# Where the memory values' tail products stand, and when a tile's mean and deviation are taken: a two-part reordering in a layer-interleaved recurrent-memory transformer kernel

## The chip, the cores and the metric

The kernel runs on one core of one Trainium2 chip. The metric is the device time of one execution in microseconds (us). One core has five engines: TensorE (PE, with its weight loads shown separately as PEld), VectorE (DVE), ScalarE (ACT), GpSimd (POOL) and SyncE (SP, which only issues DMAs here). The engines run on their own and meet at semaphores. Each engine takes its instructions in order. TensorE writes its products into PSUM, a memory that this kernel uses as eight banks; ScalarE and VectorE copy them out, and in this program a bank takes new products only when its last reader is done.

## The reference, cut to what matters

Two attention layers with a recurrent memory and two gated MLP layers are stacked, and the weights are shared:

```python
x = x + A(layernorm(x)); x = x + B(layernorm(x))
x = x + A(layernorm(x)); x = x + B(layernorm(x))

# A: 64 segments of 32 rows; each sees 8 memory rows that the segment before it has made
h = concat([mem, xs]); q, k, v = h @ Wq, h @ Wk, h @ Wv        # 16 heads of 256
o = softmax(mask(q k^T * scale)) v @ Wo
mem = o[:8]; outs.append(o[8:])
# B: (relu(x @ W_gate) * (x @ W_up)) @ W_down, 448 -> 1792 -> 448
```

x is 2048 x 448 in bf16. The memory makes A sequential in the segments.

## The kernel before

It works in 70 steps, one segment per step. Chain C1 is the first A layer and C2 the second, six segments behind. In steps 6 to 63 both chains run together, in one set of products ("two-chain steps", 58 of them). B's work for a finished tile of 128 rows is cut into pieces (`fill`) that are dealt out into holes of TensorE. A tile is four segments, so the steps repeat in fours; I call them step 0, 1, 2 and 3 by their number modulo four. C1 ends a tile in step 3, C2 in step 1.

The order within a two-chain step: `G = M h` in bank pairs (TensorE into PSUM, copied out by ScalarE and VectorE); scores `S = G h`; softmax on VectorE and ScalarE; values `vps = B h`; products with the weights (`AT_ps`); memory rows back into `hTr` (`mps`).

Width 448 is 3 x 128 + 64. The last 64 rows are the "tails": a tail product uses only 64 rows of the array, and two of them, from the lower and the upper half, can run at once (eight value tails of 448 columns take 0.20 us below, while fourteen full products of 448 columns take 2.82 us, 0.20 us each). Two tails from different halves must not write one PSUM bank together, so the score tails go in two turns with a fence in between: GpSimd waits for the last score tail of the first turn and writes a token, and TensorE waits for the token.

```python
def pass_on():
    op = nc.gpsimd.memset(token[:], 0.0)
    sync(op, last_of[nc.tensor.engine])      # waits for TensorE's last matmul
    return op.ins.name
...
def dual(g, chains, inG, mid, ...):
    gp.run(inG); G = gp.G
    matmul(SX[:, 0:N], selq[LO], maskb[LO], start=True, ...)    # the mask product
    mid()                                    # one or two relu pieces of B
    ...
    vm.part(0, True)                         # 8 value tails, banks 0 and 1
    for e in range(2):
        for k in range(4):
            x_tails(k, e)                    # score tails: bank SX, half e
            m_tails(k, 1 - e)                # bank SM, the other half
        if not e:
            passed = pass_on()
            vm.part(1, True)                 # 8 value tails, banks 2 and 3
            fence.append(passed)             # the next matmul waits for the token
    ... full score products, softmax, values ...
    end()                                    # a relu piece ("first product" below)
    ... mps, copies into hTr ...
    for c in ends:                           # a tile ends: add its rows into x
        nc.vector.tensor_tensor(x3[:, cc], ps[...], x3[:, cc], op=ALU.add)
    last()                                   # a relu piece ("second product")

# after the step, for a chain whose tile ended
f = FFN(c, t); f.norm()
```

In B:

```python
def norm(self):                              # bn_stats + bn_aggr on VectorE, rstd on GpSimd
    self.stats = ln_stats(self.t, recent.get("hh"))    # behind the last relu product
def rows(self, after):
    self.xn = ln_rows(self.stats, True, after)         # (x - mean) * rstd, twice
    nc.sync.dma_start_transpose(self.xnT[:], ...)      # transposed by DMA
def turn(self):                              # the first piece of B
    if self.xn is None:
        self.rows(recent["G1"])              # behind the first VectorE copy of G
def gate_up(self, f):                        # a relu piece: 28 matmuls
    ...
    recent["ut"] = nc.scalar.copy(ut[:], gu[1][:])
    recent["hh"] = nc.vector.scalar_tensor_tensor(out=self.hh[...], in0=gu[0][:], scalar=0.0,
                                                  in1=ut[:], op0=ALU.max, op1=ALU.mult)   # the "relu product"; it reads the bank of gate
```

`behind(a, b)` only fixes the order of two instructions on one engine. What is not fixed so is ordered by a scheduler when the program is built, and the scheduler also hands out the eight PSUM banks.

## Time and profile before

| | before |
|---|---|
| time, median of the first 3 runs | 1531.71 us (1528.56 to 1534.23) |
| profiled span | 1529.0 us |
| TensorE busy / weight loads busy | 98% / 75% |
| length of steps 0, 1, 2, 3 (mask product to mask product) | 21.92, 24.52, 21.14, 19.47 us |

The page of the kernel before begins with the span and the engines' busy time:

```profile
span 1529.0 us, 88780 instructions
PE 1492.6 (98%) x41744; PEld 1139.1 (75%) x41744; DVE 951.1 (62%) x2202; ACT 603.8 (39%) x1410; POOL 150.1 (10%) x523
```

TensorE is the engine to relieve, but its 98% hides small holes, because the ends of matmuls are modelled. The Trainium skill (Perfetto Trace Analysis, "Identifying the Most-Contended Engine") also says that matmul busy time is not a good measure of how close a kernel is to its limit, and names weight-load busy time as one of two better ones; here weight loads stand at 75%. The waits view shows who waited for whom: total us, times, longest us. Two of its lines belong to this change:

```profile
PEld L138 <- POOL token L145: 22.9, 58, 0.4
PEld L138 <- DMA xnT_1183<-xd_94: 4.0, 5, 1.1
```

The first is the fence, once in each two-chain step. The second are relu pieces that found the transposed rows of a C1 tile not yet landed.

The timeline of the fence in a step 0 whose mask product stands at 724.86 (columns: start, duration, engine, line, operation, out<-in, shapes, count, idle time before and what ended it):

```profile
724.95 1.05 DVE L501 CAST G<-gps 128x480 bf16<-128x480 f32 x2 [1.84 <-PE gps L138]
...
726.96 0.38 PE L138 MATMUL vps<-BT_sb,memTp_81 64*32 64x448 bf16 x8
727.16 0.20 PE L138 MATMUL S_ps<-G,hTr 64*32 64x80 bf16 x1
...
727.20 0.22 PE L138 MATMUL S_ps<-G,hTr 64*32 64x80 bf16 x4
727.23 0.37 PE L138 MATMUL vps<-BT_sb,memTp_81 64*32 64x448 bf16 x8
...
727.54 0.10 POOL L145 MEMSET token<- 128x1 f32 x1 [7.20 <-PE S_ps L138]
727.69 0.21 PE L138 MATMUL S_ps<-G,hTr 64*32 64x80 bf16 x1
```

Eight value tails occupy the array for 0.20 us (726.96 to 727.16). From the first score tail to the release are 0.53 us (727.16 to 727.69), and in this hole stand only eight value tails. G is complete long before, at 726.00.

The timeline of the end of a step 3, in which C1 finishes a tile (put together from the views of the single engines):

```profile
803.81 0.68 DVE L953 TENSOR_TENSOR x_ring<-AT_ps,x_ring 32x256 bf16<-32x256 f32 x2
...
804.94 0.42 DVE L352 SCALAR_TENSOR_TENSOR hh<-gate,ut 128x256 bf16<-128x256 f32 x1 [0.44 <-ACT ut L351]
804.95 0.84 PE L138 MATMUL gps<-hTr,MT_sb 64*128 64x80 bf16 x36
...
805.56 0.42 DVE L352 SCALAR_TENSOR_TENSOR hh<-gate,ut 128x256 bf16<-128x256 f32 x1 [0.19 <-ACT ut L351]
...
805.90 0.62 DVE L264 BATCH_NORM_STATS2 stats<-x_ring 128x6 f32<-128x448 bf16 x1
806.55 0.18 DVE L266 BATCH_NORM_AGGREGATE mv<-stats 128x2 f32<-128x6 f32 x1
...
807.80 0.50 DVE L282 TENSOR_SCALAR xd_94<-x_ring,mv,rstd 128x448 bf16<-128x448 bf16 x1
...
808.68 1.26 SPq L330 DMA_TRANSPOSE xnT_1183<-xd_94  x1
```

The rows are added by 804.49; then VectorE idles 0.44 us until ScalarE delivers `ut`; then come the two relu products, and the statistics only behind both. The DMA leaves 4.87 us after the add began. The 36 G tails of the next step run without a visible wait at 804.95, three bank pairs of twelve. The third pair reuses the bank that the first relu product reads: its second product starts 0.05 us after that relu product ends.

### The profile page before, as it was taken

To read this page: it belongs to the slowest core of one execution; us is meant where nothing else is said; L and a number is where in the kernel's file an instruction comes from. 1 tells how busy PE (TensorE), PEld (TensorE's weight loads), DVE (VectorE), ACT (ScalarE), POOL (GpSimd) and SP (SyncE) were. 2 spreads that over 40 slices of the span, in tenths; PEclk is the share of its full clock that TensorE was granted. 3 is DMA by queue.
4 is the path that set the end of the run, shared out by engine and by line. 5 is a ranking of instruction groups with operands and counts; after the bars stand their busy time and mean duration, and the time that the engine had idled before them with its cause. 6 is when DMAs were issued, how large, how long until landed. Compare 5 with 4: busy or idle time off the path is not lost. (4 is left out here: it accounts for less than half of the span.)

```text
span 1529.0 us, 88780 instructions
## 1 busy us (share of the span) xinstructions
PE 1492.6 (98%) x41744; PEld 1139.1 (75%) x41744; DVE 951.1 (62%) x2202; ACT 603.8 (39%) x1410; POOL 150.1 (10%) x523
## 2 busy tenths in 40 slices
PE   7999999999999999999999999999999999999998
PEld 4577777778777787778778777877778777777775
DVE  6645566666666666666666666666666665666444
ACT  5644333434343343434344343434334343433443
POOL 2001001010100011010100101010001100001000
PEclk9999999999999999999999999999999999999999
DMA  9731001010000100010000100000000000000000
GB/s 237 168 99 35 5 14 14 12 20 13 20 7 15 18 12 21 12 21 13 9 18 15 19 12 20 12 22 6 15 18 12 18 11 15 12 6 14 5 7 9
DMA packets 82798, 39.35 MB, mean 26 GB/s; under 512 B 65176, under 2 KB 81536, under 8 KB 82432
## 3 DMA queue, kind: packets, MB, share of 16 engines
q1 hardware_dynamic: 82400, 33.68, 10.3%
q8 instruction: 326, 5.34, 1.5%
q14 instruction: 40, 0.33, 0.1%
q10 hardware_dynamic: 32, 0.01, 0.0%
HBM read 14.00 MB, written 1.84 MB: 10 GB/s over the span
## 5 line engine op out<-in xcount | busy, mean ns | idle before, releaser
L138 PE MATMUL gps<-hTr,M_sb 128*128 128x80 bf16 (+1 forms) x11760 | 415.3, 198 | 2.1 <-issue 1.9
L138 PEld LDWEIGHTS <-M_sb 128*128 128x128 bf16 x11760 | 405.1, 99 | 7.2 <-issue 2.7
L501 DVE CAST G<-gps 128x480 bf16<-128x480 f32 (+4 forms) x327 | 194.4, 611 | 223.9 <-PE gps L138 223.7
L501 ACT CAST G<-gps 128x480 bf16<-128x480 f32 (+4 forms) x327 | 165.6, 525 | 344.9 <-PE gps L138 344.9
L138 PEld LDWEIGHTS <-hTr 128*32 128x32 bf16 (+2 forms) x8464 | 178.0, 94 | 164.5 <-issue 47.5
L138 PE MATMUL vps<-B_sb,hTr 128*32 128x448 bf16 x4464 | 235.6, 353 | 0.0
L138 PEld LDWEIGHTS <-Wgu 64*128 64x128 bf16 x6272 | 184.1, 94 | 24.4 <-issue 19.3
L425 ACT CAST vox<-vps 128x448 bf16<-128x448 f32 x186 | 96.1, 533 | 181.1 <-PE vps L138 181.1
L352 DVE SCALAR_TENSOR_TENSOR hh<-gate,ut 128x256 bf16<-128x256 f32 x224 | 94.1, 420 | 69.2 <-ACT ut L351 69.2
L425 ACT CAST VOm<-vps 128x448 bf16<-128x448 f32 x251 | 120.5, 526 | 14.8 <-PE vps L138 14.7
L351 ACT CAST ut<-up 128x256 bf16<-128x256 f32 x224 | 83.8, 374 | 70.3 <-PE up L138 70.3
L425 DVE CAST vox<-vps 128x448 bf16<-128x448 f32 x186 | 104.9, 600 | 9.0 <-PE vps L138 9.0
L853 ACT ACTIVATE se<-se 128x320 f32<-128x320 f32 x116 | 54.5, 470 | 129.4 <-DVE se L852 129.4
L138 PE MATMUL gate<-xnT_1182,Wgu 64*128 64x128 bf16 x1568 | 103.5, 216 | 0.9 <-DMA xnT_1182<-xd_93 0.6
L138 PE MATMUL up<-xnT_1182,Wgu 64*128 64x128 bf16 x1568 | 103.6, 216 | 0.0
L138 PE MATMUL gate<-xnT_1183,Wgu 64*128 64x128 bf16 x1568 | 99.1, 216 | 3.8 <-DMA xnT_1183<-xd_94 2.7
L138 PE MATMUL up<-xnT_1183,Wgu 64*128 64x128 bf16 x1568 | 99.2, 216 | 0.0
L138 PEld LDWEIGHTS <-TW 128*32 128x32 bf16 x3712 | 90.7, 97 | 11.1 <-DVE TW L883 0.7
L138 PE MATMUL gps<-hTr,MT_sb 64*128 64x80 bf16 (+1 forms) x3920 | 92.1, 196 | 3.0 <-ACT hTr L946 0.7
L138 PEld LDWEIGHTS <-memTp_81 128*32 128x32 bf16 (+1 forms) x2820 | 67.0, 95 | 36.3 <-issue 1.7
L138 PEld LDWEIGHTS <-memTp_83 128*32 128x32 bf16 (+1 forms) x2820 | 67.2, 95 | 35.1 <-issue 0.6
L138 PE MATMUL dps<-Wd,hh 128*128 128x448 bf16 x448 | 92.7, 354 | 0.0
(194 smaller groups left out, 1730.8 us busy)
## 6 DMA issues: line engine op xcount, KB each, us to landing
wo<-in_A_Wo_dram SPq DMA_DIRECT2D x8, 448.0 KB, 5.1
out_dram<-x_ring SPq DMA_DIRECT2D x16, 112.0 KB, 1.7
Wgu<-in_B_W_gate_dram SPq DMA_DIRECT2D x7, 224.0 KB, 3.3
Wgu<-in_B_W_up_dram SPq DMA_DIRECT2D x7, 224.0 KB, 3.5
Wd<-in_B_W_down_dram SPq DMA_DIRECT2D x7, 224.0 KB, 3.1
wvn_124<-in_A_Wv_dram SPq DMA_DIRECT2D x4, 384.0 KB, 3.5
wvn_125<-in_A_Wv_dram SPq DMA_DIRECT2D x4, 384.0 KB, 5.9
x_ring<-in_A_x_dram SPq DMA_DIRECT2D x10, 112.0 KB, 3.0
```

Source lines behind the costliest of these rows:

```text
L138: op = nc.tensor.matmul(*a, **k)
L351: recent["ut"] = nc.scalar.copy(ut[:], gu[1][:])
L352: recent["hh"] = nc.vector.scalar_tensor_tensor(out=self.hh[:, f:f + 2, :], in0=gu[0][:], scalar=0.0, in1=ut[:], op0=ALU.max, op1=ALU.mult)
L425: op = self.evac[2 * x + e](self.dst[:, 2 * e + x, :], self.ps[x][e][:, 0:DM])
L501: op = (cp_a, cp_v)[self.side](gp.G[:, self.side, self.t0:self.t0 + self.n, gp.c0:gp.c1, :], self.ps[:, 0:self.n * gp.NP].rearrange("p (m ...
L853: vm.after = nc.scalar.activation(se[:, q], se[:, q], AF.Exp, scale=SCALE)
```

## The change

The intent: (A) put both value-tail passes into the hole of the fence. (B) Take the C1 tile's statistics right after the rows are added, make its normalized rows ahead of the next step's first G copy, and so send the transposing DMA earlier.

```diff
 # ln_rows
-            nc.vector.tensor_copy(xd[:, :, 1], xd[:, :, 0])
+            recent["rows"] = nc.vector.tensor_copy(xd[:, :, 1], xd[:, :, 0])
 # FFN.norm
-            self.stats = ln_stats(self.t, recent.get("hh"))
+            self.stats = recent.pop("stats", None) or ln_stats(self.t, recent.get("hh"))
 # Bank.out, first VectorE copy of G
                 if not self.t0:
                     recent["G1"] = op
+                    if ahead_of_G:
+                        behind(op, ahead_of_G.pop())
+    ahead_of_G = []
 # dual
-        vm.part(0, True)
         for e in range(2):
             for k in range(4):
                 x_tails(k, e)
                 m_tails(k, 1 - e)
             if not e:
                 passed = pass_on()
-                vm.part(1, True)
+                vm.both(True)
                 fence.append(passed)
 # dual, behind the add of an ended tile's rows
+            if c is C1:
+                recent["stats"] = ln_stats((g - c.lag) // 4)
 # after the step
                 if c is C2 and recent["two"] and g + 1 < nseg and t:
                     f.rows(recent["sum"])
+                elif c is C1 and recent["two"] and g + 1 < nseg:
+                    f.rows(recent["hh"])
+                    ahead_of_G.append(recent["rows"])
```

## The prediction

> **What bounds it now.** The page: TensorE 98% busy of a 1529.0 us span, weight loads 75%, VectorE 62%, granted clock 0.999. The Trainium skill (Perfetto Trace Analysis, "Identifying the Most-Contended Engine") judges TensorE by weight loads, not matmuls; either way only gaps of its in-order stream can be saved. The waits view gives the two that this change touches: weight loads behind the token, 22.9 us in 58 waits; behind the DMA into xnT_1183, 4.0 us in 5.
>
> **Step A, both tail passes between the turns.** 58 two-chain steps have the fence. The skill (TensorEngine Tiling, "Gotcha 1: PSUM Pressure") says row tiles must not write one bank together: hence the fence; no run here tests it. In the timeline of a step with two relu pieces ahead: value tails start 1.79 us after the mask matmul, first score tails 1.99, second value tails 2.06, token 2.37, release 2.53. The release follows the first score tail by 0.54 us whatever fills it; eight value tails fill only 0.2. Moving the other eight into the hole starts score tails 0.20 earlier. Nothing is removed or added.
> - Steps 0 and 1 of each four (28): G is ready at 1.15, long before. Saved 28 x 0.20 = 5.6 us.
> - Steps 2 and 3 (30): one relu piece. Tails start 1.01, VectorE's last G cast ends 1.15, score tails start 1.21: the eight tails were hiding that cast. The k=3 score tails will now wait for it; saved about 30 x 0.04 = 1.2 us.
> A: -6.8 us, all on TensorE's stream.
>
> **Step B, statistics and rows of a C1 tile earlier.** VectorE work is unchanged: 0.62 + 0.18 us statistics, 0.50 + 0.29 rows. Now the transposing DMA is issued about 3.2 us after the relu product and lands 2.9 to 4.6 us later; where it is late, the relu matmuls wait: five tiles, 3.7 us together beyond the usual. Issued 1.0 to 1.5 us earlier, those waits go: -3.7 us.
> Cost: VectorE is idle only 0.44 us before the first relu product, so the statistics push it 0.15 to 0.37 us. In the timeline the third bank pair's tails of the next step start 0.04 us after this product ends, at its release: no slack. 15 tile ends x 0.15 to 0.37 = 2 to 5.5 us, unless banks are handed out differently; I take +3.5 us. The rows ahead of the first G cast delay it at most 0.3 us; no bank is short there.
> B: about 0.
>
> **Sum.** -6.8 - 3.7 + 3.5 = -7.0 us: 1531.7 to 1525 us, range 1519 to 1530. Faster by over 2%: 1%; within 2%: 98%; slower: 1%.
>
> **What would show it.**
> - A: 16 value tails in one group behind the score tails; mask-to-release 2.53 to 2.33 in steps 0 and 1, 1.74/1.80 to about 1.70/1.76 in steps 2 and 3; wait for the token from 0.39 each to 0.2 and 0.1. Score tails waiting for G's cast in steps 2 and 3 only.
> - B: C1's transposing DMA issued 1.0 to 1.5 us earlier; waits on xnT_1183 from 4.0 to under 0.5 us; the relu product at C1 ends later by 0.15 to 0.37 us, and a TensorE wait of that size before the third pair's tails.
>
> **What would make it wrong.** Token latency depending on the queue ahead (A smaller); PSUM banks handed out in another order, so the product no longer gates tails (B better) or gates earlier ones (B worse); the DMA landing late for another reason; the scheduler placing the statistics after the first product.

## The result

| | before | changed |
|---|---|---|
| time, median of 4 runs | 1531.8 us | 1526.31 us (1525.36 to 1527.48) |
| ratio (95% interval) | | 0.9966 (0.9945 to 0.9986) |
| profiled span | 1529.0 us | 1523.6 us |
| length of steps 0, 1, 2, 3, usual | 21.92, 24.52, 21.14, 19.47 us | 21.73, 24.33, 21.06, 19.73 us |

A ratio is the mean time of one kernel's fast runs over that of the other's in the same rounds, so it isn't quite the ratio of the medians quoted.

Steps 0, 1 and 2 became shorter, step 3 became longer by 0.26 us. Two-chain steps together are 6.8 us shorter (here and below: the 56 from step 6 to step 61, mask product to mask product). The page and the waits of the changed kernel (the second line from the view of TensorE alone):

```profile
span 1523.6 us, 88780 instructions
PE 1494.2 (98%) x41744; PEld 1143.1 (75%) x41744; DVE 952.3 (63%) x2202; ACT 603.8 (40%) x1410; POOL 149.4 (10%) x523
```

```profile
PEld L138 <- POOL token L145: 15.2, 58, 0.3
PE gps L138 <- DVE hh L352: 2.3, 13, 0.2
```

Busy times tell nothing: TensorE is even 1.6 us busier and its weight loads are 4.0 us busier, in a shorter span. The waits tell it. The token costs 15.2 us instead of 22.9. The line for the DMA into xnT_1183 is gone. A new line stands there: G products waiting for a relu product, in 13 steps. The view counts only 0.2 us for each, since earlier matmuls were still modelled as running.

The fence in the same step 0, whose mask product now stands at 723.24:

```profile
723.33 1.06 DVE L501 CAST G<-gps 128x480 bf16<-128x480 f32 x2 [1.84 <-PE gps L138]
...
725.03 0.21 PE L138 MATMUL S_ps<-G,hTr 64*32 64x80 bf16 x1
...
725.07 0.23 PE L138 MATMUL S_ps<-G,hTr 64*32 64x80 bf16 x4
725.11 0.58 PE L138 MATMUL vps<-BT_sb,memTp_81 64*32 64x448 bf16 x16
...
725.42 0.10 POOL L145 MEMSET token<- 128x1 f32 x1 [8.21 <-PE S_ps L138]
...
725.57 0.21 PE L138 MATMUL S_ps<-G,hTr 64*32 64x80 bf16 x1
```

The score tails lead, 16 value tails stand in one group behind them, and first score tail to release is 0.54 us again (725.03 to 725.57). From the mask product to the release it is 2.33 us; in a step 0 without a late DMA it was 2.53.

The end of a step 3 in the changed kernel:

```profile
801.35 0.68 DVE L955 TENSOR_TENSOR x_ring<-AT_ps,x_ring 32x256 bf16<-32x256 f32 x2
...
802.06 0.63 DVE L264 BATCH_NORM_STATS2 stats<-x_ring 128x6 f32<-128x448 bf16 x1
802.48 0.63 PE L138 MATMUL gps<-hTr,MT_sb 64*128 64x80 bf16 x25
...
802.73 0.18 DVE L266 BATCH_NORM_AGGREGATE mv<-stats 128x2 f32<-128x6 f32 x1
802.83 0.74 DVE L352 SCALAR_TENSOR_TENSOR hh<-gate,ut 128x256 bf16<-128x256 f32 x2
...
803.28 0.37 PE L138 MATMUL gps<-hTr,MT_sb 64*128 64x80 bf16 x11 [0.17 <-DVE hh L352]
...
803.90 0.51 DVE L282 TENSOR_SCALAR xd_94<-x_ring,mv,rstd 128x448 bf16<-128x448 bf16 x1 [0.34 <-POOL rstd L269]
...
804.80 1.26 SPq L330 DMA_TRANSPOSE xnT_1183<-xd_94  x1
```

The DMA now leaves 3.45 us after the add began, 1.42 earlier. The first relu product starts 1.48 us after the add began, 0.35 later than before (1.13). The 36 G tails are cut into 25 and 11: the 26th, the third pair's VectorE bank, waits for that product.

### The profile page after: what moved, and what is told of

The parts are those of the page before. It is cut to its first block, busy times and chain, and to the rows that moved or that the text cites. A ratio compares the mean times of both kernels' runs of the same rounds, so it can differ in the third digit from the quotient of the medians.

```text
span 1523.6 us, 88780 instructions
## 1 busy us (share of the span) xinstructions
PE 1494.2 (98%) x41744; PEld 1143.1 (75%) x41744; DVE 952.3 (63%) x2202; ACT 603.8 (40%) x1410; POOL 149.4 (10%) x523
## 4 chain that ended last, share of the span: by engine, by line
PE 93%; DVE 3%; SPq 1%; DMA 1%; issue 1%; ACT 1%; POOL 0%; POOLq 0%; ACTq 0%
PE gps L138 32%; PE vps L138 29%; PE gate L138 8%; PE S_ps L138 6%; PE AT_ps L138 6%; PE dps L138 6%; PE up L138 3%; PE ps L138 2%; SPq L181 1%; DMA wq<-in_A_Wq_dram 1%; DVE stats L264 1%; DVE x_ring L955 1%; PE yt L138 0%; PE mps L138 0%; PE tps L150 0%
```

## The experiments

The theory has three separate terms: A saves in every fence, B saves the late DMAs, B costs a stall as long as the delay of the first relu product. Rival 1: the loss in step 3 comes from A's reordering. Rival 2: the DMA waits went because A shifted the stream. The kernels of the first four experiments shared the runs of before on one chip (11 runs, median 1529.47 us, 1526.48 to 1533.53); the later four had the same and one more.

### Step A alone

Edit: the change without every line of B.

```diff
-        vm.part(0, True)
         for e in range(2):
...
-                vm.part(1, True)
+                vm.both(True)
```

> Step A alone (both value-tail passes between the banks' turns; statistics and rows of a C1 tile as before). Theory (three separate terms): mask-to-release falls 0.19-0.20 us in steps 0 and 1 and about 0.07 in steps 2 and 3, the length of step 3 (mask of step 3 to mask of the next step 0) falls by 0.07 and shows no 0.33 us stall, the five late-DMA waits on xnT_1183 stay (about 3.7 us in total beyond the usual); sum -7.6 us against before, ratio about 0.995. Rival 1 (the 0.33 us that step 3 lost comes from the new place of the value tails, not from the statistics): step 3 is 0.26 us longer here as in the changed kernel, sum about -3.5 us. Rival 2 (the DMA waits went because step A shifted the stream): the waits on xnT_1183 are gone here.

Measured: 1521.42 us (6 runs), ratio 0.9953 (0.9938 to 0.9968). Mask-to-release fell 0.19 us in steps 0 and 1 and 0.07 to 0.08 in steps 2 and 3; step 3 fell by 0.08, so its loss isn't A's. Two-chain steps together fell by 7.3 us. The late DMAs stayed; the waits view of this kernel (in my own kernels the buffer numbers are missing from the names):

```profile
PEld L138 <- POOL token L145: 15.2, 58, 0.3
PEld L138 <- DMA xnT<-xd: 4.6, 6, 1.2
```

Both rivals fail here: no stall in step 3, and the DMA waits remain. A alone is at least as fast as the whole change.

### Step B alone

Edit: the changed kernel with the value tails put back.

```diff
+        vm.part(0, True)
         for e in range(2):
...
-                vm.both(True)
+                vm.part(1, True)
```

> Step B alone (statistics ahead of the relu products, rows ahead of the first G cast; value tails as before). Theory: waits on xnT_1183 gone (-3.7 us), relu product at C1 ends 0.36 us later and 0.33 us of TensorE stall before the third bank pair's tails in 13 to 15 steps (+4.3 to +5 us), sum about +0.9 us, ratio about 1.0006, i.e. step B by itself is worth nothing. Rival 1: no stall in step 3, sum -3.7 us, ratio 0.9976. Rival 2: the waits on xnT_1183 stay, sum +4.6 us, ratio 1.003.

Measured: 1529.99 us, ratio 1.0005 (0.9990 to 1.0020). In the five steps 0 with a late DMA 3.7 us are gone, in thirteen steps 3 4.4 us are added (0.34 each), and all other full steps stayed to 0.01 us, apart from step 10 (0.7 us shorter, the first C2 tile's DMA, which comes out differently in every run). The waits view of this kernel:

```profile
PEld L138 <- POOL token L145: 22.9, 58, 0.4
PE gps L138 <- DVE hh L352: 2.3, 13, 0.2
```

B by itself is worth nothing: its gain and its cost cancel.

### The statistics between the two relu products

Edit to the changed kernel: the statistics are put behind the first product.

```diff
-                recent["stats"] = ln_stats((g - c.lag) // 4)
+                recent["stats"] = ln_stats((g - c.lag) // 4, recent.get("hh"))
```

> The changed kernel with the C1 statistics put between the two relu products of the step's end instead of ahead of both. Theory: the first relu product is back at its old time after the add (no TensorE wait on it, step 3 falls by 0.33 us in 14 steps, -4.6 us against the changed kernel); the transposing DMA is issued about 0.5 us earlier than before instead of 1.4, so of the five late landings about 1.4 us of waits in total come back; the second relu product is about 0.6 us later and nothing waits on it. Sum about -3.2 us against the changed kernel, about -9 us against before, ratio about 0.994. Rival 1 (the loss in step 3 is not the relu product's delay): no change in step 3, not faster than the changed kernel.

Measured: 1519.67 us, ratio 0.9930 (0.9914 to 0.9947). Two-chain steps are 10.9 us shorter than before. The end of a step 3 in this kernel:

```profile
803.77 0.42 DVE L352 SCALAR_TENSOR_TENSOR hh<-gate,ut 128x256 bf16<-128x256 f32 x1 [0.44 <-ACT ut L351]
803.78 0.84 PE L138 MATMUL gps<-hTr,MT_sb 64*128 64x80 bf16 x36
...
804.11 0.62 DVE L264 BATCH_NORM_STATS2 stats<-x_ring 128x6 f32<-128x448 bf16 x1
...
806.84 1.36 SPq L330 DMA_TRANSPOSE xnT<-xd  x1
```

The 36 G tails are whole again and step 3 is 0.07 shorter than before, as in A alone. The add began at 802.65, so the DMA leaves 4.19 us after it, 0.68 earlier than before; I had expected 0.5. Of the late landings about 0.8 us of waits came back (0.29, 0.16 and 0.35 us in steps 16, 24 and 32), not the 1.4 expected: my size was off, for the earlier issue and because other tiles were late in this run. The second relu product is 0.47 us later, and the first G copy 0.64 us later, and neither costs anything.

### Only the aggregation behind the first product

Edit to the changed kernel: `bn_aggr` (0.18 us) behind the first product, `bn_stats` ahead of it.

```diff
-        nc.vector.bn_aggr(mv[:], stats[:])
+        behind(nc.vector.bn_aggr(mv[:], stats[:]), aggr_after)   # the first relu product
```

> The changed kernel with only the aggregation (0.18 us) put behind the first relu product; the 0.63 us of statistics stay ahead of it. Theory (the stall is as long as the product's delay): the first relu product is delayed by 0.15 to 0.18 us instead of 0.36, the TensorE stall before the third pair's tails falls from 0.33 to about 0.15, -2.5 us in 14 steps against the changed kernel; the DMA still leaves about 1.0 us earlier than before, so no waits on xnT_1183. Sum about -2.5 us against the changed kernel, ratio to before about 0.995. Rival 1: step 3 unchanged, same time as the changed kernel.

Measured: 1520.72 us, ratio 0.9943 (0.9926 to 0.9960). The product is 0.14 us late, and the first full G product behind the tails comes 0.12 us late. No DMA of a C1 tile is waited for. Two-chain steps are 9.8 us shorter than before.

### The suspected cost doubled

Edit to the changed kernel: `bn_stats` of a C1 tile runs twice.

```diff
         behind(nc.vector.bn_stats(stats[:], xt), after)
+        if twice:
+            nc.vector.bn_stats(stats[:], xt)
```

> The changed kernel with the suspected cost doubled: the 0.63 us of statistics of a C1 tile run twice in a row ahead of the relu products; results stay right. Theory (no slack: every ns of delay of the first relu product is a ns of TensorE stall): the product is 0.65 us later than in the changed kernel, the stall before the third pair's tails grows from 0.33 to about 0.98 us, step 3 is 0.65 us longer in 13 or 14 steps: +8.5 to +9.1 us against the changed kernel, ratio to before about 1.002. Rival (the stall comes from another wait that only happens to lie there): step 3 as in the changed kernel, same time.

Measured: 1531.94 us (4 runs), ratio 1.0017 (1.0001 to 1.0034). Step 3 is 0.92 us longer than before in all thirteen. The end of a step 3 in this kernel:

```profile
807.93 0.73 DVE L354 SCALAR_TENSOR_TENSOR hh<-gate,ut 128x256 bf16<-128x256 f32 x2
...
808.39 0.37 PE L138 MATMUL gps<-hTr,MT_sb 64*128 64x80 bf16 x11 [0.84 <-DVE hh L354]
```

The four kernels make a line, with nothing between cause and effect:

| | delay of the first relu product | delay of the first full G product |
|---|---|---|
| statistics between the products | 0.00 | 0.00 us |
| only the aggregation behind | 0.14 | 0.12 |
| changed kernel | 0.35 | 0.33 |
| statistics twice | 1.01 | 1.00 |

Both are measured from the start of the step's first copy out of `AT_ps`, against before (1.71 and 2.49 us there), as medians of 13 steps. There is no slack: in all ten kernels run here, the kernel before among them, the 26th G tail starts 0.052 to 0.054 us after the end of the first relu product. The 0.02 us between the two columns is the product itself, which takes 0.405 us where it is delayed and 0.425 us before.

### Both value-tail passes ahead of the score tails

Edit to the kernel before, the reverse of A:

```diff
-        vm.part(0, True)
+        vm.both(True)
...
                 passed = pass_on()
-                vm.part(1, True)
```

> The kernel before with step A reversed: both value-tail passes stand ahead of the first score turn, none between the turns; results stay right. Theory (the release follows the first score tail by 0.54 us whatever stands in the hole, and a pass ahead of it costs 0.20): in steps 0 and 1 first score tails 2.19 us after the mask matmul and release 2.73 (0.20 later than before), in steps 2 and 3 first score tails at 1.41 and release about 1.94; the wait for the token grows from 0.39 to about 0.6 us each; 56 steps x 0.20 = +11 us against before, ratio about 1.007. Rival (the release is set by the value tails or by TensorE's queue, so the hole is not a fixed latency): release unchanged or earlier, same time as before.

Measured: 1541.79 us (4 runs), ratio 1.0080 (1.0060 to 1.0099). The release came 0.19 us later in every step from 8 on in which no late DMA interfered. In steps 6 and 7, which have no relu piece behind the mask product, it stayed at 1.67 and 1.73 us, here as in A alone: there the last score tails wait for the last copy of G, wherever the value tails stand. The waits view of this kernel:

```profile
PEld L138 <- POOL token L145: 25.2, 58, 0.5
```

So 0, 8 and 16 value tails in the hole give releases of 2.72, 2.53 and 2.33 us after the mask product in steps 0 and 1: 0.19 to 0.20 us a pass. The weight-load wait grew less than I had expected (0.43 us each, not 0.6), since it starts at the last weight load and not at the last matmul; the size of such a wait isn't the size of the hole.

### Repeats of the best and of the changed kernel

No edit; the same two kernels beside each other, 6 runs each.

> The statistics between the two relu products, a second time, beside the changed kernel on the same chip. From the first trace: two-chain steps 10.9 us shorter than before against 6.8 us for the changed kernel; so ratio to before 0.993, and about 4 us (0.3%) ahead of the changed kernel, less or more by an extra half-clock stretch of 3.4 us (1.5 us of work) that falls in some executions. Rival (the first result was luck of the chip and of those stretches): no difference to the changed kernel.

Measured: 1518.44 us, ratio 0.9929 (0.9913 to 0.9945); two-chain steps again 10.9 us shorter than before.

> The changed kernel itself, as the yardstick for the statistics between the products: ratio to before 0.9955 to 0.9966; the same trace as the first time in every two-chain step (0.19, 0.07 us saved, 0.26 lost in step 3, no waits on xnT_1183). The half-clock stretch inside the last relu matmuls, if chance of the start, is gone or elsewhere.

Measured: 1524.46 us, ratio 0.9964 (0.9949 to 0.9978). The two intervals don't touch, so the statistics between the products beat the changed kernel, by 0.35% of the time of before. Step for step the changed kernel's two-chain trace is that of the first time, apart from step 10 (0.41 us longer) and step 60 (0.09 us shorter).

This pair also settled a puzzle. In the first profile of the changed kernel the last relu pieces ran at half speed. Windows over the beginning of these pieces, first before, then changed (columns: stretch, length, busy us and count of PE, PEld, DVE, ACT, POOL, then granted clock, DMA share, GB/s):

```profile
1517.00:1520.00 3.00, 2.79 (x100) 2.78 (x101) 0.85 (x2) 1.14 (x4) 0.00 (x0) 1.00 0.14 44
```

```profile
1510.00:1513.00 3.00, 2.75 (x53) 2.74 (x54) 0.42 (x1) 0.58 (x2) 0.00 (x0) 0.54 0.13 44
```

There are 53 matmuls where before has 100, at a granted clock of 0.54. The clock's record has one stretch of 3.413 us at 0.5, from 1510.2. The second profile of the changed kernel hasn't got it there, and its span is 1519.6 us, not 1523.6: 1.9 of these 4.0 us lie behind the last mask product (25.27 and 23.34 us to the end), where the stretch was, and most of the rest in steps 63 to 69. So the stretch isn't a fixed cost of the change. Step B alone and the repeated best kernel have one there too. Whether the change makes it likelier isn't shown: of the ten profiles three have it there, all among the seven of kernels that hold B.

One thing could not be tried: a fence without GpSimd, TensorE waiting for its own last score tail. Built so, no wait comes out on TensorE; it didn't run.

## Why the prediction was right or wrong, point by point

- **The total.** Predicted 1525 us, 7.0 less than before; measured 1526.31, and a ratio of 0.9966 (5.2 us of 1531.8), the second time 0.9964. Right. The terms, from the traces: A -7.3 us in two-chain steps, late DMAs -3.7, stall 13 x 0.33 = +4.3; together -6.7, and two-chain steps fell by 6.8. The whole runs gained less. In the first profile 1.9 us go to the half-clock stretch; why the mean of the runs is also 1.5 us short of -6.7 isn't settled, since the parts outside differ by more than that from profile to profile: the time up to the first two-chain step takes 162.1 to 166.9 us, and steps 63 to 69 differed by 2.2 us between two profiles of the changed kernel.
- **A in steps 0 and 1.** Predicted 2.53 to 2.33 and 5.6 us; measured 2.33 and 28 x 0.19 = 5.3. Right, and shown in both directions: a pass moved out of the hole costs 0.19.
- **A in steps 2 and 3.** Predicted 1.74/1.80 to 1.70/1.76 (1.2 us); measured 1.67/1.73 (27 x 0.075 = 2.0 us). The mechanism is right: the first score tails now start at 1.01, the last at 1.24, behind the G copy that ends at 1.15. The term was mis-sized, 0.04 for 0.075 us: I let the whole 0.54 us of the fence follow the copy of G, but only the last three of the twelve score tails wait for it (from 1.20 us on), and from there to the release it is 0.47 us in step 2. The kernel before shows this limit already, in its steps 6 and 7: release at 1.67 and 1.73 us, as now in all steps 2 and 3. I predicted the token wait as 0.2 and 0.1 us; it is 0.22 and 0.18 in steps 0 and 1, but 0.28 and 0.35 in steps 2 and 3: I had taken the weight-load wait for the hole.
- **The late DMAs.** Predicted -3.7 us with an issue 1.0 to 1.5 us earlier; measured 1.41 earlier, no wait left, -3.7. Right, and shown to be B's work.
- **The stall.** Predicted: the first relu product 0.15 to 0.37 us later, a TensorE wait as long before the third pair's tails, +3.5 us. Measured: 0.35, 0.33, +4.3 us. The mechanism is right and shown by four doses; I took the middle of the range where the scheduler gave the top, because it put the aggregation ahead of the product too.
- **"The rows ahead of the first G cast delay it at most 0.3 us; no bank is short there."** That copy starts 0.33 us later in the changed kernel, all of it TensorE's own stall. With the statistics between the products it starts 0.64 us later at no cost, so no bank is short there even then.

The row rule behind the fence is in the Trainium skill (TensorEngine Tiling (Array Packing), "Gotcha 1: PSUM Pressure"): different row tiles may not access one PSUM bank at the same time, and software must synchronize. No run here breaks it.

What stays open: why the transposing DMA lands 2.9 us after its issue in some steps and up to 4.8 in others, and why the fence takes 0.06 us more in steps 3 than in steps 2. And the hole isn't closed: in steps 0 and 1 the last group of value tails ends about 0.08 us before the release (an estimate: the second eight start at 2.06 us, a pass takes 0.19, the release is at 2.33).

## What to carry to other kernels

A fence whose round trip does not depend on what stands in it (0.53 to 0.54 us here with 0, 8 or 16 value tails, in steps 0 and 1) is a place to put work into. Moving work from ahead of it to behind it gains that work's whole time, as long as the hole has room for it and the products that now start earlier have their inputs ready; where they haven't, the work ahead was hiding another wait. Before an idle moment of a helper engine is filled, look at what the bottleneck takes from that engine next: here 0.8 us of VectorE work in a 0.44 us hole stood ahead of a product that frees a PSUM bank, and the stall ate what the earlier DMA had won. One position later the same work was free, so try the neighbouring positions of a moved instruction, not only "early" and "late".

## What the Trainium skill lacked or had wrong

- TensorE: Matmul & The Clock Gate ("Part 1: The HAM clock gate") gives a window of 3413 ns for the gate, at half rate or full. The runs agree: every complete stretch at 0.5 lasts 3.413 or 3.414 us (107 ns from one gate matmul to the next instead of 56). It says that the half rate follows an idle window. Here it began at 1510.2 us in the changed kernel when no window had been wholly idle: TensorE's last gaps were 0.86 and 0.99 us, with a 0.56 us group of transposes between them. These gaps alone don't decide it: the kernel before has 0.85 and 0.99 us in the same place and stayed at full clock. Two pairs of profiles of one kernel, with and without the stretch behind the last mask product, differ there by 1.9 and 1.6 us. The page's part on PSUM-queue cycling does tell of a clock that drops after short idles, but gives no number for such part-idle windows.
- No page that I found gives the time of a TensorE to GpSimd to TensorE round trip: 0.53 to 0.54 us in steps 0 and 1 from the start of the 12 score tails of the first turn to the release (0.12 to 0.13 from the modelled end of the last tail to the token, 0.10 the token, 0.05 to TensorE's start); in steps 3 of the kernel before it is 0.59.
- DMA: Bandwidth & Descriptors ("DMA Transpose (X-bar)") has no landing time for a small transpose within SBUF: 2.9 to 4.8 us from issue to landing for 128 x 896 bf16 here, with 1.2 to 2.8 us of it on the issuing queue.
- Perfetto Trace Analysis ("Tensor Engine Instruction") says that the ends of matmuls are estimated. It follows, and the page doesn't say so, that a wait counted from there comes out too small: 0.17 us was shown for a stall of 0.33 us.
